# Splitting the gates' logarithms into two float32r numbers for the prefix sums of a gated linear attention

## The chip, the core and the metric

The kernel runs on one core of a Trainium2 chip. A core has five engines, each with its own instruction queue: PE (matrix products; its weight loads are listed apart as PEld), DVE (VectorE, elementwise work and reductions), ACT (ScalarE, activation functions and copies), POOL (GpSimd, some elementwise work and DMA issue) and SP (SyncE, DMA issue here). The metric is the device time of one execution in microseconds (us), the median over runs. Less is better.

## The reference

A linear attention with a forget gate feeds a mixture of experts with two levels of gates. Cut to what matters here:

```python
# q, k, v, f_logit: (4 batches, 8 heads, 768 steps, 48)
f = 1.0 / (1.0 + np.exp(-f_logit))
for t in range(S):
    state = f[:, :, t, :, None] * state + np.einsum('bhd,bhe->bhde', k[:, :, t], v[:, :, t])
    y[:, :, t] = np.einsum('bhd,bhde->bhe', q[:, :, t], state)
x = y.transpose(0, 2, 1, 3).reshape(3072, 384)
# 4 groups of 4 experts; each token goes to one group and one expert in it
h = np.maximum(x_of_expert @ w1[g, e], 0.0)      # 384 -> 1024
out[tokens] = weight * (h @ w2[g, e])            # 1024 -> 384
```

## The kernel before

**Stages.** The first 140 us or so are the attention stage, the rest the experts. Routing (which expert a token goes to) runs beside the attention, and the experts' weights are loaded while it ends.

**Units and passes.** The 768 steps are cut into 6 chunks of 128, the 4 batches into 2 pairs. A unit is a chunk and a pair: units 0 to 11, of 128 steps on the partitions and 2 x 8 x 48 = 768 columns. Inside a unit the recurrence is done with matrix products. They need, for each step, the sum of the logarithms of the gates from the chunk's first step to it. Unit i goes through these stages, each a Python generator whose yields split it into steps:

- c (`bounded`, L577): DVE clamps the loaded f logits in place (L581).
- g (`gated`, L584): ACT takes Exp (L591), then Ln (L594), so that `nl` holds the negative logarithm of the gate. Then, for each of the two batches, PE multiplies by the upper triangle `tri` of ones, which makes the sums over steps, `cs` (L600, a float32 product of 128x128 with 128x384), and ACT takes two Exps of it, `eq` (L601) and `kh` (L602). After the second batch a small DMA (L607) writes `ends`.
- m (`multiplied`): DVE multiplies q by `eq` (L620) and makes `kh` from it and k (L623).
- t (`turned`): PE transposes both (L634), ACT copies them out (L635).
- s (`scored`): PE makes the scores `ap` (L659), DVE masks them with `tri` into `am` (L662).
- n (`stated`): PE makes the state's increment `ds` (L676); DVE updates the state (`sp` L682, `st` L683).
- w (`weighed`): PE makes the outputs (L697 from the state, L701 from `am`), ACT copies them (L704).
- d, x, b: the gates' logits (`lT` L717, `lgT` L719, `lg` L722, `lgs` L723), the rows of x (L742 to L750), and the decays (`gt` L643, `decays` L644).
- r: one step of the routing of the oldest finished chunk (`route`, L178). Its DVE chain makes, among others, `pick` (L211), the places `at` (L220), `ln` (L226), `val` (L233), `meta` (L244) and `table` (L256). PE takes `val` in `tb` (L251). POOL sends `meta` by DMA (L246).

**Order.** The order on PE, DVE, ACT and SP is written out by hand: the sequence of steps is the order in which each of these engines gets its instructions, and each queue runs in that order. POOL's instructions are placed by the scheduler. A list `BEGIN` starts the first units. From `BEGUN = 3` to 11, pass i runs the list for i (`EVEN` or `ODD`, or an entry of `ORDERS`); a token such as `g+1` means the next step of stage g of unit i+1. In pass i the clamp of unit i+2 comes right after the masks of unit i, its Exp and Ln come between the later steps, and the sums of unit i+1 (`g+1 g+1`) come before the masks:

```python
EVEN = "l+2 d-2 n-1 r r r x-1 x-1 t t t t g+1 g+1 x-1 r s s s s c+2 w d-1 g+2 w g+2 n m+1 m+1".split()
```

So the sums of unit 5, the sixth, run in pass 4, and those of unit 11 in pass 10. Routing's chain from `pick` to `table` lies in the even passes.

**Loads.** Token `l+2` of pass i makes SP ask for k and q of unit i+2, f of unit i+3 and v of unit i+2 (L575). The tile of f has three buffers, and so the load of f of a unit waits until the unit three before has no further reader.

Of the kernel before, what the change touches and what calls it, by code (L numbers as in the profile page):

```python
# [10 lines left out]
FP32 = mybir.dt.float32  # L11
I32 = mybir.dt.int32
U32 = mybir.dt.uint32
BF16 = mybir.dt.bfloat16
AF = mybir.ActivationFunctionType
OP = mybir.AluOpType
AX = mybir.AxisListType.X
ET = mybir.EngineType
P = 128
# [4 lines left out]
def kernel(  # L24
# [12 lines left out]
    nc = tc.nc  # L37
    B, H, S, D = q.shape
# [38 lines left out]
    def const(shape, dtype, name):  # L77
        return cp.tile(shape, dtype, tag=name, name=name)

    def bank(shape, name):  # L80
        return ps.tile(shape, FP32, tag="bank", name=name)
# [7 lines left out]

    tri = const([P, P], FP32, "tri")  # L90
    ident = const([P, P], FP32, "ident")
    strictb = const([P, P], BF16, "strictb")
    onesb = const([P, P], BF16, "onesb")
    halves = const([P, 2], FP32, "halves")
    make_upper_triangular(nc, tri, val=1.0, diag=True)
    make_identity(nc, ident)
    nc.vector.memset(onesb, 1.0)
    nc.vector.tensor_tensor(strictb, tri, ident, OP.subtract)


# [43 lines left out]
    part = const([P, NC, B, 2], FP32, "part")  # L144
    partb = const([P, NC, B, 2], BF16, "partb")

# [23 lines left out]
    def rows_of(c, s=0, n=B):  # L170

        first = 1 + (c * B + s) * P
        return x_dram[first:first + n * P, :].rearrange("(b p) w -> p b w", p=P)
# [4 lines left out]
    def route(c, lg, sb, tabled=True, tidy=None, counted=None, ranking=None):  # L178


        def tmp(shape, name, dtype=FP32, bufs=1):
            return sb.tile(shape, dtype, tag=name, bufs=bufs, name=name)
# [13 lines left out]
        ohv = oh.rearrange("p (n a) e -> p n a e", n=B)  # L196
        ohe = tmp([P, B, GE], "ohe", BF16)
        nc.vector.tensor_tensor(ohe.rearrange("p n (g e) -> p n g e", e=EG), ohv[:, :, 1:G + 1, :],
# [5 lines left out]
        for n in range(B):  # L204
            nc.tensor.matmul(rk[:, n + 1:, :], lhsT=onesb, rhs=ohe[:, n:n + 1, :].broadcast_to((P, B - n, GE)), start=False, stop=(n == B - 1), skip_group_check=True)
        nc.scalar.activation(dl, dl, AF.Exp)
        yield
# [10 lines left out]
        if tabled:  # L218
# [5 lines left out]
            nc.vector.tensor_copy(atf, at)  # L224
            ln = tmp([P, B, P], "ln", BF16)
            nc.vector.tensor_tensor(ln, lanes.unsqueeze(1).broadcast_to((P, B, P)), atf[:, :, 0:1].broadcast_to((P, B, P)), OP.is_equal)  # L226
# [3 lines left out]
            nc.vector.tensor_tensor(head, heads_of.rearrange("p e j -> p (e j)").unsqueeze(1).broadcast_to(BLK), atf[:, :, 1:2].broadcast_to(BLK), OP.is_equal)  # L230
            val = tmp([P, 2, B, 2 * GE], "val", BF16)
            for m in range(2):
# [199 lines left out]
    def up(w, w1):  # L432
        n = w["n"]
        w["h"] = h = room(w, FO, "h")
        for f in range(0, FO, 2):
            hp = bank([P, 2, n], "hp")
            for o in range(2):
                for ko in range(KO):
                    nc.tensor.matmul(hp[:, o, :], lhsT=w1[:, ko, (f + o) * P:(f + o + 1) * P], rhs=w["xT"][:, ko, :], start=(ko == 0), stop=(ko == KO - 1))  # L439
            nc.scalar.activation(h[:, f:f + 2, :], hp, AF.Relu)  # L440
            yield

    def put(w, j, m, yp):

        y = w["pool"].tile([P, DM], FP32, tag="yt", bufs=2 if w["pool"] is ep else 4, name="yt")
        if w["n"] == P or "rows" in w:
            nc.scalar.activation(y[0:m], yp[0:m], AF.Copy, scale=w["x"][0:m, j, DM:DM + 1])  # L447
        else:
# [70 lines left out]
    with ExitStack() as fast:  # L519
        sb = fast.enter_context(tc.tile_pool(name="sb", bufs=2))  # L520
# [26 lines left out]
        NU = len(units)  # L547

        CORNERS = [(b, h) for b in range(2) for h in range(2)]
        KEPT = NU - 4  # L550
        live = {}
        groups, ends = {}, {}

        def heads(t):
            return t.rearrange("p b h d -> p (b h) d")

        def side(i):


            return nc.gpsimd if i < NU - 2 else nc.scalar  # L560
# [3 lines left out]
        def parts(i):  # L564

            return (slice(0, 1), slice(1, 2)) if i == 0 else (slice(0, 2),)

        def load(i, names):
            c, s = units[i]
            w = live.setdefault(i, {"v": pads["v"][i % 4], "qh": pads["qh"][i % 3]})  # L570
            for nm in names:
                if nm not in w:
                    w[nm] = sb.tile([P, 2, H, D], FP32, tag="ld_" + nm, bufs=3 if nm == "f" else 2, name="ld_" + nm)
                for b in parts(i) if nm == "f" else (slice(0, 2),):
                    nc.sync.dma_start(out=heads(w[nm][:, b])[:, :, 0:D], in_=SRC[nm][2 * s + b.start:2 * s + b.stop, :, c * P:(c + 1) * P, :].rearrange("b h t d -> t (b h) d"))  # L575
# [8 lines left out]
        def gated(i):  # L584

            c, s = units[i]
            w = live[i]

            nl = w["f"].rearrange("p b h d -> p b (h d)")
            for b in parts(i):  # L590
                nc.scalar.activation(nl[:, b], nl[:, b], AF.Exp, bias=0.0, scale=-1.0)  # L591
                if i:
                    yield
                nc.scalar.activation(nl[:, b], nl[:, b], AF.Ln, bias=1.0, scale=1.0)  # L594
            eq, qh, kh = pads["eq"][i % 2], w["qh"], pads["kh"][i % 3]
            w.update(eq=eq, kh=kh)
            yield
            for b in range(2):
                cs = bank([P, H, D], "cs")
                nc.tensor.matmul(cs.rearrange("t h d -> t (h d)"), lhsT=tri, rhs=nl[:, b], start=True, stop=True)  # L600
                nc.scalar.activation(eq[:, b, :, 0:D], cs, AF.Exp, bias=0.0, scale=-1.0)  # L601
                nc.scalar.activation(kh[:, b, :, 0:D], cs, AF.Exp, bias=0.0, scale=1.0)  # L602
                if b:

                    if s == 0:
                        ends[c] = sb.tile([B * HP, P], FP32, tag="ends", bufs=1, name="ends")
                    side(i).dma_start(out=ends[c][2 * HP * s:2 * HP * (s + 1), :], in_=eq[P - 1:P].rearrange("o b (a r) d -> o (b a) (r d)", r=2))  # L607
                yield
# [120 lines left out]
        def listed(i):  # L729

            c, s = units[i]
            xT = live[i]["xT"]
            if i < KEPT:
                if i % 4 == 0:
# [4 lines left out]
            for b in range(2):  # L739
# [8 lines left out]
                yield  # L748
            if i >= KEPT:
                side(i).dma_start(out=rows_of(c, 2 * s, 2)[:, :, 0:DM], in_=x.rearrange("t b a r d -> t b (a r d)"))  # L750
# [4 lines left out]
        def send_kept():  # L755

            for j, t in enumerate(rows_kept):
                nc.sync.dma_start(out=rows_of(2 * j, 0, 2 * B)[:, :, 0:DM], in_=t)
# [20 lines left out]
        def advance(gens):  # L779
            if gens and next(gens[0], True):  # L780
                gens.pop(0)
# [5 lines left out]

        STAGES = {"c": bounded, "g": gated, "m": multiplied, "t": turned, "s": scored, "n": stated, "w": weighed, "d": done, "x": listed, "b": decayed}
        BEGIN = """c0 g0 p g0 g0 m0 m0 m0 m0 l2 t0 t0 t0 t0 h c1 g1 g1 s0 s0 s0 s0 g1 g1 p w0 w0 n0 m1 m1 m1 m1 l3 h x0 x0 x0
            t1 t1 t1 t1 b1 c2 g2 g2 s1 s1 s1 s1 p d0 g2 g2 n0 n1 w1 w1 m2 m2 l4 n1  # L790
            d0 x1 x1 t2 t2 t2 t2 c3 g3 g3 x1 s2 s2 s2 s2 w2 g3 g3 d1 w2 n2 m3 m3 c4 g4 g4""".split()
        BEGUN = 3
        EVEN = "l+2 d-2 n-1 r r r x-1 x-1 t t t t g+1 g+1 x-1 r s s s s c+2 w d-1 g+2 w g+2 n m+1 m+1".split()
        ODD = "l+2 d-2 r r x-1 x-1 t t t t b n-1 g+1 g+1 x-1 r s s s s c+2 w d-1 g+2 w g+2 n m+1 m+1 r n".split()
        ORDERS = {
            NU - 3: "l+2 o d-2 r r x-1 x-1 t t t t b n-1 r g+1 g+1 x-1 r s s s s c+2 w d-1 g+2 w g+2 n m+1 m+1 r n".split(),
            NU - 2: "d-2 r x-1 x-1 r t t t t r g+1 g+1 x-1 s s s s w d-1 w n m+1 m+1".split(),
            NU - 1: "d-2 r r n-1 x-1 x-1 t t t t r x-1 r s s s s w b d-1 w r r".split(),
            NU: "d-2 r e d-1 x-1 x-1 d-1 x-1 r r r e e r e r r e r r e r e r r e e e e e".split(),
# [3 lines left out]
        def step(nm, i):  # L803
            if nm == "r":
                advance(routes)
            elif nm == "e":
                next(first[0], None)
            elif nm == "p":
                next(pad)
            elif nm == "o":  # L810
                send_kept()
            elif nm == "h":
                next(turning)
            elif 0 <= i < NU:
                if nm == "l":

                    load(i, ("k", "qh"))
                    if i + 1 < NU:
                        load(i + 1, ("f",))
                    load(i, ("v",))  # L820
                    return
                if (nm, i) not in steps_of:
                    steps_of[nm, i] = STAGES[nm](i)
                next(steps_of[nm, i], None)
# [14 lines left out]
        for i in range(BEGUN, NU + 1):  # L839
            if i == BEGUN:  # L840
                nc.sync.dma_start(out=x_dram[0:1, 0:DM].rearrange("o (h d) -> o h d", d=D), in_=blank[:, 0:D].unsqueeze(1).broadcast_to((1, H, D)))
                nc.sync.dma_start(out=x_dram[0:1, DM:RW], in_=blank[:, D:D + 2])
            for tok in ORDERS.get(i, ODD if i % 2 else EVEN):
                step(tok[0], i + int(tok[1:] or 0))
# [39 lines left out]
    ahead = {n: load_weights(wq if n % 3 == 1 else wp, who[0:1, PLACES[n]:PLACES[n] + 1]) for n in range(1, 2)}  # L884
# [22 lines left out]
    for n in range(GE - 1):  # L907
        w = ws[n]
# [105 lines left out]
    with tc.If(more > 0), ExitStack() as late:  # L1014
# [5 lines left out]
        with tc.For_i(0, last, 1) as i:  # L1020
            w1, w2 = load_weights(wp, b_expert[0:1, bass.ds(i, 1)])
# [13 lines left out]
            w = fetch(ep, row, P, late=True)  # L1035
# [32 lines left out]
```

## Time and profile before

| | us |
|---|---|
| median of 3 runs | 416.83 |
| the runs | 415.68 to 417.15 |
| the profiled execution, device time | 415.58 |
| its span in the trace | 413.8 |

| group (line, engine) | count | mean ns | busy us |
|---|---|---|---|
| `cs` product, L600 PE (two instructions a product) | 48 | 486 to 510 | 18.6 |
| expert product `hp`, L439 PE | 864 | 320 | 138.6 |
| expert product `yo`, L475 PE | 672 | 333 | 115.8 |
| masks `am`, L662 DVE | 48 | 682 | 29.8 |
| `qh` product, L620 DVE, 128x768, from 50 to 125 us | 7 | 949 | 6.6 |
| Exp, L591 ACT, 128x768, from 50 to 125 us | 6 | 844 | 5.1 |
| Ln, L594 ACT, 128x768, from 50 to 125 us | 6 | 849 | 5.1 |

A line of the profile's groups gives line, engine and operation, the tiles written and read, the shape, the count, then the busy time and the mean duration of one, and last the idle time of the engine before them with what ended it. Matrix products overlap each other, so their mean duration is longer than the distance between two of them. The timeline lists instructions of one engine by start and length; the chain of waits lists, in order of time, what the end of the program depended on. From 50 to 110 us PE was busy in every stretch of 10 us, DVE between 6.42 and 9.29 us of each, ACT between 6.81 and 7.39.

### The profile page before, as it was taken

The page shows a single profiled execution, that of the slowest core. Times are in us where ns is not written, and L with a number is a line of the kernel's source. Part 1 is how long each engine was busy: PE and PEld are TensorE (multiplying, and loading weights), DVE is VectorE, ACT ScalarE, POOL GpSimd, SP SyncE. Part 2 cuts the span into 40 slices and gives each one's busy share as a digit, 9 for nine tenths or more (in the row PEclk, how much of TensorE's full clock was granted, in tenths as well). Part 3 has the DMA queues.
Part 4 walks back from the last instruction along what each step waited for, and adds up shares of the span by engine and source line. Part 5 has one row for each costly group of instructions (what it writes and reads, how often), then busy time and mean ns, then how long its engine had stood idle before and what let it go on. Part 6 is the DMA issues. An engine that isn't in the chain of part 4 may idle for free.

```text
span 413.8 us, 10066 instructions
## 1 busy us (share of the span) xinstructions
PE 405.5 (98%) x4047; PEld 374.6 (91%) x4047; DVE 267.0 (65%) x778; ACT 157.1 (38%) x353; POOL 83.2 (20%) x127
## 2 busy tenths in 40 slices
PE   8999999999999999999999999999999999999995
PEld 3888888888778978889999999999999999999992
DVE  6666787878898722630899768486595595584230
ACT  6777766666565312221213122222232232231220
POOL 4000010101012157001042221311321320120230
PEclk9999999999999999999999999999999999999999
DMA  9999997877999559974829468486496596485010
GB/s 174 199 202 212 190 185 146 153 141 153 318 346 391 165 192 351 391 276 160 298 68 332 150 230 280 143 326 205 175 349 180 208 347 200 182 320 163 28 47 24
DMA packets 132145, 88.98 MB, mean 215 GB/s; under 512 B 102582, under 2 KB 122748, under 8 KB 132090
## 3 DMA queue, kind: packets, MB, share of 16 engines
q1 hardware_dynamic: 125666, 75.50, 62.1%
q0 software_dynamic: 5792, 11.92, 9.4%
q10 hardware_dynamic: 632, 0.83, 0.6%
q8 instruction: 34, 0.56, 0.5%
q14 instruction: 21, 0.17, 0.1%
HBM read 78.71 MB, written 9.83 MB: 214 GB/s over the span
## 4 chain that ended last, share of the span: by engine, by line
PE 48%; issue 30%; DMA 10%; POOL 6%; DVE 4%; POOLq 1%; ACT 1%; SPq 0%
PE hp L439 12%; DMA out_dram<-yt,xg 7%; PE yo L475 7%; PE ap L659 5%; PE y L701 5%; PE yo L460 4%; POOL out_dram L450 4%; PE cs L600 3%; POOL xg L393 2%; PE x_ps L742 2%; PE ds L676 2%; PE tr_k L634 2%; DMA xg<-x_dram,rows_e 2%; PE tr_q L634 2%; PE y L697 2%
## 5 line engine op out<-in xcount | busy, mean ns | idle before, releaser
L439 PE MATMUL hp<-xe,w 128*128 128x128 f32 (+14 forms) x864 | 138.6, 320 | 0.0
L439 PEld LDWEIGHTS hp<-xe,w 128*128 128x128 f32 x864 | 135.8, 190 | 0.8
L422 DVE STREAM_TRANSPOSE yr<-yT 32x192 f32<-32x192 f32 (+1 forms) x208 | 70.5, 339 | 70.4 <-ACT yT L476 67.8
L475 PE MATMUL yo<-h,w 128*128 128x230 f32 (+13 forms) x672 | 115.8, 333 | 0.0
L475 PEld LDWEIGHTS yo<-h,w 128*128 128x128 f32 x672 | 113.7, 190 | 0.2
L415 DVE STREAM_TRANSPOSE xe<-xg 32x192 f32<-32x192 f32 (+1 forms) x208 | 69.7, 335 | 8.6 <-PE hp L439 5.6
L440 ACT ACTIVATE h<-hp 128x256 f32<-128x256 f32 (+14 forms) x72 | 34.4, 478 | 103.5 <-PE hp L439 103.5
L450 POOL DMA_INDIRECT out_dram<-yt,xg x32 | 34.4, 1076 | 149.2 <-ACT yt L447 143.7
L476 ACT COPY yT<-yo 128x230 f32<-128x230 f32 (+13 forms) x42 | 13.5, 326 | 80.5 <-PE yo L475 80.5
L393 POOL DMA_INDIRECT xg<-x_dram,rows_p x30 | 29.6, 986 | 52.7 <-DMA out_dram<-yt,xg 29.7
L662 DVE TENSOR_TENSOR am<-ap,tri 128x512 f32<-128x512 f32 x48 | 29.8, 682 | 10.8 <-PE ap L659 10.8
L701 PE MATMUL y<-am,v 128*64 128x128 f32 x384 | 24.4, 276 | 0.2
L701 PEld LDWEIGHTS y<-am,v 128*64 128x64 f32 x384 | 20.9, 137 | 3.3 <-issue 1.8
L659 PE MATMUL ap<-Tq,Tk 48*64 48x128 f32 x768 | 23.8, 272 | 0.0
L659 PEld LDWEIGHTS ap<-Tq,Tk 48*64 48x64 f32 x768 | 20.8, 133 | 1.6 <-issue 1.1
L460 PE MATMUL yo<-w,h 128*128 128x384 f32 x64 | 21.3, 486 | 0.0
L460 PEld LDWEIGHTS yo<-w,h 128*128 128x128 f32 x64 | 11.9, 190 | 7.4
L600 PE MATMUL cs<-ld_f,tri 128*128 128x384 f32 x48 | 18.6, 510 | 0.0
L607 POOL DMA_DIRECT2D ends<-eq x10 | 5.4, 541 | 55.5 <-ACT eq L601 55.5
L447 ACT ACTIVATE yt<-yr,xg 128x384 f32<-128x384 f32 (+13 forms) x26 | 14.4, 604 | 5.4 <-DVE yr L422 5.4
L704 ACT COPY xT<-y 128x512 f32<-128x512 f32 x24 | 13.5, 581 | 4.5 <-PE y L701 4.4
L634 PE MATMUL tr_q<-ident,qh 128*128 128x128 f32 x96 | 14.5, 274 | 0.5 <-issue 0.5
(173 smaller groups left out, 369.5 us busy)
## 6 DMA issues: line engine op xcount, KB each, us to landing
w<-in_moe_w_dram SPq DMA_DIRECT2D x34, 1536.0 KB, 11.0
qh<-in_q_dram SPq DMA_DIRECT2D x12, 384.0 KB, 5.3
ld_k<-in_k_dram SPq DMA_DIRECT2D x12, 384.0 KB, 6.0
v<-in_v_dram SPq DMA_DIRECT2D x12, 384.0 KB, 5.8
ld_f<-in_f_logit_dram SPq DMA_DIRECT2D x11, 384.0 KB, 5.8
x_dram<-x_kept SPq DMA_DIRECT2D x2, 1536.0 KB, 11.1
x_dram<-x POOLq DMA_DIRECT2D x2, 384.0 KB, 6.9
x_dram<-x ACTq DMA_DIRECT2D x2, 384.0 KB, 8.1
```

The source lines that it names most:

```text
L393: nc.gpsimd.indirect_dma_start(out=w["x"][:, j, :], out_offset=None, in_=x_dram[0:1 + top, :], in_offset=bass.IndirectOffsetOnAxis(ap=rows ...
L415: squares(w, lambda n, k_, rk, g, rg: nc.vector.transpose(out=xT[rg, 0:n, k_], in_=x[rk, 0:n, g]))
L422: squares(w, lambda n, k_, rk, g, rg: nc.vector.transpose(out=y[rk, 0:n, g], in_=yT[rg, 0:n, k_]))
L439: nc.tensor.matmul(hp[:, o, :], lhsT=w1[:, ko, (f + o) * P:(f + o + 1) * P], rhs=w["xT"][:, ko, :], start=(ko == 0), stop=(ko == KO - 1))
L440: nc.scalar.activation(h[:, f:f + 2, :], hp, AF.Relu)
L450: sent = nc.gpsimd.indirect_dma_start(out=out, out_offset=bass.IndirectOffsetOnAxis(ap=w["x"][0:m, j, DM + 1:RW].bitcast(U32), axis=0), in ...
L460: nc.tensor.matmul(yp, lhsT=w["h"][:, fo, :], rhs=w2[:, fo, :], start=(fo == 0), stop=(fo == FO - 1))
L475: nc.tensor.matmul(yp, lhsT=w2[:, fo, m * P:(m + 1) * P], rhs=w["h"][:, fo, :], start=(fo == 0), stop=(fo == FO - 1))
L600: nc.tensor.matmul(cs.rearrange("t h d -> t (h d)"), lhsT=tri, rhs=nl[:, b], start=True, stop=True)
L634: nc.tensor.transpose(out=pt[:, a, :], in_=w[nm + "h"][:, b, 2 * a:2 * a + 2, :].rearrange("t r d -> t (r d)"), identity=ident)
L659: nc.tensor.matmul(ap[r][half, a, :], lhsT=w["Tk"][rows, b, a, half], rhs=w["Tq"][rows, b, a, :], start=True, stop=True)
L701: nc.tensor.matmul(ys[b][DP * h:DP * h + DP, a, :], lhsT=w["v"][:, b, 2 * a + (b ^ h), :], rhs=w["am"][b][:, b ^ h, a, :], start=(c == 0 a ...
```

## The change

From unit 5 on (`SPLIT = 5`), `nl` is split into two tiles of type float32r, in a step of its own: `most` is a rounded copy that ACT writes, `least` the rest, `nl - most`, that POOL writes. PE multiplies both by `trir`, the triangle as float32r, and adds the two products in the same `cs`. The tiles `most` and `least` have one buffer each. The constant `trir` is one more DVE copy at the start.

The order changes with it. In pass i the split of unit i+2 and Exp and Ln of unit i+3 stand before the masks (`g+2 g+3 g+3`), and the clamp of unit i+4 stands last (`c+4`), behind `qh` and `kh` of unit i+1. Pass 3 has a list of its own that catches up: clamps of units 5, 6 and 7, Exp and Ln of units 5 and 6, split of unit 5. The load of f moves a unit ahead: a new token `f6` stands in `BEGIN` behind `l4`, and from `l5` on the load of f is that of two units after, so that `l5` asks for f of unit 7.

```diff
@@ const
+    trir = const([P, P], F32R, "trir")
...
+    nc.vector.tensor_copy(trir, tri)
@@ gated
+            pieces = [nl]
+            if i >= SPLIT:
+                pieces = [sb.tile([P, 2, H * D], F32R, tag=nm, bufs=1, name=nm) for nm in ("most", "least")]
+                nc.scalar.copy(pieces[0], nl)
+                nc.gpsimd.tensor_tensor(pieces[1], nl, pieces[0].bitcast(FP32), OP.subtract)
+                yield
             for b in range(2):
                 cs = bank([P, H, D], "cs")
-                nc.tensor.matmul(cs.rearrange("t h d -> t (h d)"), lhsT=tri, rhs=nl[:, b], start=True, stop=True)
+                for n, piece in enumerate(pieces):
+                    nc.tensor.matmul(cs.rearrange("t h d -> t (h d)"), lhsT=trir if i >= SPLIT else tri, rhs=piece[:, b], start=(n == 0), stop=(n == len(pieces) - 1))
@@ orders
-            t1 t1 t1 t1 b1 c2 g2 g2 s1 s1 s1 s1 p d0 g2 g2 n0 n1 w1 w1 m2 m2 l4 n1
+            t1 t1 t1 t1 b1 c2 g2 g2 s1 s1 s1 s1 p d0 g2 g2 n0 n1 w1 w1 m2 m2 l4 f6 n1
-        EVEN = "l+2 d-2 n-1 r r r x-1 x-1 t t t t g+1 g+1 x-1 r s s s s c+2 w d-1 g+2 w g+2 n m+1 m+1".split()
-        ODD = "l+2 d-2 r r x-1 x-1 t t t t b n-1 g+1 g+1 x-1 r s s s s c+2 w d-1 g+2 w g+2 n m+1 m+1 r n".split()
+        EVEN = "l+2 d-2 n-1 r r r x-1 x-1 t t t t g+1 g+1 x-1 r g+2 g+3 g+3 s s s s w d-1 w n m+1 m+1 c+4".split()
+        ODD = "l+2 d-2 r r x-1 x-1 t t t t b n-1 g+1 g+1 x-1 r g+2 g+3 g+3 s s s s w d-1 w n m+1 m+1 c+4 r n".split()
         ORDERS = {
-            NU - 3: "l+2 o d-2 r r x-1 x-1 t t t t b n-1 r g+1 g+1 x-1 r s s s s c+2 w d-1 g+2 w g+2 n m+1 m+1 r n".split(),
+            BEGUN: "l+2 d-2 r r x-1 x-1 t t t t b n-1 g+1 g+1 c+2 x-1 r g+2 g+2 g+2 s s s s c+3 w d-1 g+3 w g+3 n m+1 m+1 c+4 r n".split(),
+            NU - 3: "l+2 o d-2 r r x-1 x-1 t t t t b n-1 r g+1 g+1 x-1 r g+2 s s s s w d-1 w n m+1 m+1 r n".split(),
@@ step
                 if nm == "l":
+                    ahead = i + 1 if i < BEGUN + 2 else i + 2
                     load(i, ("k", "qh"))
-                    if i + 1 < NU:
-                        load(i + 1, ("f",))
+                    if ahead < NU:
+                        load(ahead, ("f",))
                     load(i, ("v",))
                     return
+                if nm == "f":
+                    load(i, ("f",))
+                    return
```

More of the change, by code (lines that the diff above doesn't have):

```diff
@@ L14 @@
 BF16 = mybir.dt.bfloat16
+F32R = mybir.dt.float32r
 AF = mybir.ActivationFunctionType
@@ L550 @@
         KEPT = NU - 4
+        SPLIT = 5
         live = {}
```

## The prediction

> **What bounds the kernel now.** I read the page's first part, then the chain of waits from 40 to 125 us, then the timelines of DVE and SP where that chain leaves PE, then the groups by shape for prices. Busy shares first:
>
> ```profile
> PE 405.5 (98%) x4047; PEld 374.6 (91%) x4047; DVE 267.0 (65%) x778; ACT 157.1 (38%) x353; POOL 83.2 (20%) x127
> ```
>
> PE is the bound over the span, but a share is a mean over stages. The chain in the attention stage (columns: start, length, what) shows how thin the margin to DVE is:
>
> ```profile
> 51.87 1.29 PE cs L600 x4
> 53.16 0.12 PE tb L251 x4
> 53.28 1.91 PE ap L659 x64
> ...
> 73.14 1.29 PE cs L600 x4
> 74.43 0.12 PE tb L251 x4
> 74.55 1.91 PE ap L659 x64
> ...
> 115.88 0.56 DVE st L683
> 116.44 0.15 DVE lgs L723
> 116.58 0.21 DVE head L230
> 116.79 0.02 issue
> 116.82 0.51 DVE val L233 x2
> 117.32 0.05 issue
> 117.37 0.29 PE tb L251 x4
> ```
>
> Up to 102 us the chain is PE alone: each unit's cs costs 1.29 us (1.29 to 1.49). From 102.8 to 117.3 it is ACT and DVE, and PE waits at tb for val. The DVE timeline shows that even-numbered passes come close to this everywhere:
>
> ```profile
> 47.62 0.95 DVE L623 SCALAR_TENSOR_TENSOR kh<-kh,ld_k 128x768 f32<-128x768 f32 x1
> 48.49 0.21 DVE L211 TENSOR_TENSOR pick<-rk,run 128x64 f32<-128x64 f32 x1
> ...
> 52.16 0.49 DVE L233 TENSOR_TENSOR val<-head,part 128x128 bf16<-128x128 f32 x2
> ...
> 54.35 2.48 DVE L662 TENSOR_TENSOR am<-ap,tri 128x512 f32<-128x512 f32 x4 [0.27 <-PE ap L659]
> ```
>
> From 43.89 to 54.08 DVE never idles. val ends at 52.65 and PE's tb starts at 53.00 in the timeline: 0.35 us of slack, 0.30 after the 0.05 that the handover took at 117.3. The same gap stands at 74.27 and 95.68 (val ends 73.92 and 95.34). So whatever PE saves in an even pass beyond 0.30 us is given to waiting for val.
>
> **The change part by part.**
>
> *The sums.* Seven units (5 to 11) trade two float32 products for four float32r ones, each one instruction where float32 takes two. The trace has no float32r product. From above: the float32 instruction itself, 1.29/4 = 0.322 us for 384 columns; then four cost 1.29 and nothing is saved. From below: tb, bf16, 64 columns in 0.12/4 = 0.030 us, so 0.18 us for 384 and 0.72 for four. I take 0.18, since a rounded number read once resembles bf16 more than a float32 that is read twice: 0.57 us saved a unit, 4.0 over seven if PE were the bound throughout.
>
> [...]
>
> *The split.* ScalarE's copy is like L594, 128x768, 849 ns. It and the moved Exp and Ln (2.5 us together) fall into ACT's wait for lT (2.36 us idle before 67.51); lgT gets some 0.15 us late, hidden by the 0.71 us for which DVE waits for lg. Uncovered, that 0.15 would be paid a unit. GpSimd's subtraction is priced from the rows nearest to it:
>
> ```profile
> L890 POOL MEMSET yT<- 128x384 f32 x2 | 0.8, 442 | 0.0
> masks.py:199 POOL TENSOR_SCALAR_AFFINE_SELECT ident<-ident 128x128 f32<-128x128 f32 x1 | 0.3, 282 | 0.0
> ```
>
> 442/384 x 768 = 0.88 us, 282/128 x 768 = 1.69 us, and double that, 3.4, were each input to cost a pass. I take 1.7, as the select also reads SBUF. PE uses the result some 5 us later, so its own time is free. In POOL's queue the subtractions of units 6, 8 and 10 stand behind the DMA of meta (75.78) and ends (76.56), starting near 77.1, still 6 us before their use at 83.8; nothing urgent is behind them.
>
> What it may cost is DVE's. In pass 5 ACT ends dl's Exp at 65.15, the copy at 65.97, the subtraction at 67.67; earlier sums advance that by only the 0.17 us that eq waited for cs, to 67.50, while the masks (end 67.56) move by 0.57, to 66.99. If DVE's qh and kh products cannot run beside GpSimd, qh is c = 0.5 us late, in the odd passes, whose DVE chain runs straight into val. No row shows the two together: c lies between 0 and 0.5, and 2.2 with the 3.4 us subtraction. I take 0.5.
>
> [...]
>
> *The loads and the clamp.* Here I see the main cost. Pass 3 (42 to 53 us) must catch up two units: clamp 5 runs ahead of its masks (in 0.94 us of idle), clamp 6 after them, clamp 7 last, behind kh. The load of f 6 moves up, behind v 4; f 7 takes its place. The SP queue (columns: start, length) is full there, since it issues without a gap from 0.7 to 55 us:
>
> ```profile
> 38.05 1.46 SPq L575 DMA_DIRECT2D v<-in_v_dram  x1
> 39.61 1.71 SPq L841 DMA_DIRECT2D x_dram<-blank  x1
> 41.43 0.31 SPq L842 DMA_DIRECT2D x_dram<-blank  x1
> 41.84 0.39 SPq L575 DMA_DIRECT2D ld_k<-in_k_dram  x1
> 42.32 1.57 SPq L575 DMA_DIRECT2D qh<-in_q_dram  x1
> 43.99 1.86 SPq L575 DMA_DIRECT2D ld_f<-in_f_logit_dram  x1
> 45.91 2.86 SPq L575 DMA_DIRECT2D v<-in_v_dram  x1
> ```
>
> With f 6 put in at 39.6, f 7 has exactly the loads before it that v 5 has now; v 5 starts at 45.91 and lands after 6.0 us, so f 7 lands near 51.9. DVE reaches clamp 7 at 48.49 and, being in order, waits 3.4 us; clamp takes 0.47. Queued behind it are pick to val, 48.49 to 52.65 = 4.16 us. So val ends at 51.9 + 0.47 + 4.16 = 56.53, and PE's tb starts at 56.58, not 53.00: +3.58 us, with the sixth unit's saving swallowed. In later passes f is asked for 2 us after the previous kh ends (82.05 against 80.2), lands 5.8 us later, and is clamped after the next kh, 10 us on: no wait there.
>
> *Rest.* trir's copy (0.29 us by strictb's row) hides in DVE's 0.85 us wait for the first load; without that cover it is paid once. The last two units' clamps have left the DVE chain of passes 8 to 10.
>
> **The sum**, as PE's lateness against before: pass 4 +3.58; pass 5 -0.57; pass 6 -0.30 (val limits it) + 0.5 (c); pass 7 -0.57; pass 8 -0.29 + 0.5; passes 9 and 10, DVE-bound, keep nothing of cs 10 and lose unit 11's clamp, -0.47; cs 11 comes after tb, but PE then waits anyway (0.48 us at 133.68) for the gathered rows, whose time follows DVE's meta, so 0. From there PE is busy to the end. Total +2.38 us. The profiled run took 415.58 us with a span of 413.8; it becomes 418.0. The median, 416.83, lies 1.25 above, so on that scale the forecast is **419.2**.
>
> **The rivals.** (1) *No stall in pass 4.* For it: f 7's place is read off another kernel's queue, and 48 to 50 us shows DMA at only 0.49 of its share. Against: seven issues back to back. The +3.58 becomes -0.30, total -1.5, or -2.5 with c = 0: 414.3 to 415.3. This is the other side; it decides if f 7 lands before 48.5. (2) *float32r at 0.322 us.* Nothing saved; masks do not move, c falls to 0.1, within the slack of 0.30: 3.58 - 0.47 = +3.1, 419.9. So the rate of the new product moves the end by less than 1 us while the stall stands. (3) *GpSimd holds DVE.* Subtraction of 3.4 us, c = 2.2 in passes 5 and 7: +5.8, 422.6; it decides once the subtraction exceeds 2 us. (4) *Neither gain nor stall*: -0.47, 416.4.
>
> **How the numbers follow.** What one measurement can tell is about 0.5%, 2.1 us: below 414.75 is faster, above 418.9 slower. Forecast 0.44, its own range 418.2 (c = 0, +1.4) to 420.2: 0.26 slower, 0.18 same. Rival 1 0.30: 0.18 faster, 0.12 same. Rival 2 0.13: 0.11 slower, 0.02 same. Rival 3 0.08, slower. Rival 4 0.05, same. Sums: faster 0.18, same 0.37, slower 0.45. Range 414.2 to 421.2: it leaves out rival 3 and the tails.
>
> **What would show it.** In the changed profile: four cs instructions a unit at 0.72 us or less (else rival 2); DVE's clamp of unit 7 waiting some 3 us for ld_f near 49 to 52, then PE idle for as long before tb; the subtraction near 1.7 us and qh starting when it ends, not when the masks end; tb waiting for val again in passes 6 and 8. The prediction is wrong if f 7 has landed when DVE gets to it, or if DVE keeps ahead of tb in the even passes.

## The result and the profile after

| | before | after |
|---|---|---|
| median, us | 416.8 | 421.9 |
| the runs, us | 415.68 to 417.15 | 421.63 to 423.67 |
| the profiled execution, us | 415.58 | 421.69 |
| its span, us | 413.8 | 419.9 |

The ratio is 1.0136, with an interval of 1.0102 to 1.017: slower by 5 us. The forecast was 419.2, with 421.2 as the top of its range. First the busy shares of the page of the changed kernel:

```profile
PE 404.1 (96%) x4047; PEld 375.6 (89%) x4047; DVE 272.6 (65%) x779; ACT 163.0 (39%) x360; POOL 98.9 (24%) x134
```

PE is busy 1.4 us less than before, and the span is 6.1 longer: PE stands idle 7.5 us more. The chain of waits around pass 4 (start, length, what) answers to the lines shown of before:

```profile
45.77 6.13 DMA ld_f<-in_f_logit_dram
...
51.92 0.56 DVE ld_f L585
...
55.83 0.21 DVE head L233
...
56.06 0.51 DVE val L236 x2
56.57 0.05 issue
56.62 0.35 PE tb L254 x4
```

Here the chain was PE alone. Now it leaves PE for the load of f 7, goes on through its clamp and through all that DVE has queued behind it, to val, and comes back at tb, 3.62 us later than before (53.00 in the timeline). The timelines of DVE and of PE show who lost what (start, length; in brackets the idle time before the instruction and what ended it):

```profile
46.72 2.60 DVE L632 TENSOR_TENSOR qh<-qh,eq 128x768 f32<-128x768 f32 x1
49.23 0.95 DVE L635 SCALAR_TENSOR_TENSOR kh<-kh,ld_k 128x768 f32<-128x768 f32 x1
51.92 0.56 DVE L585 TENSOR_SCALAR ld_f<-ld_f 128x768 f32<-128x768 f32 x1 [1.74 <-DMA ld_f<-in_f_logit_dram]
```

```profile
53.26 0.66 PE L646 MATMUL tr_k<-ident,kh 128*128 128x128 f32 x4 [1.86 <-DVE run L217]
...
56.62 0.35 PE L254 MATMUL tb<-val,ln 128*128 128x64 bf16 x4 [1.93 <-DVE val L236]
56.90 3.52 PE L671 MATMUL ap<-Tq,Tk 48*64 48x128 f32 x64
```

DVE idles for f 7 for 1.74 us only, because qh before it took 2.60 us and not 0.95. PE idles twice, and then ap takes 3.52 us where it always took 1.98. The stretch of that ap in the windows (start and end, length, busy time of PE, PEld, DVE, ACT and POOL with instruction counts, granted clock, DMA share, which can come out above 1 for a short stretch, GB/s) says why:

```profile
57.00:58.00 1.00, 1.00 (x20) 1.00 (x24) 0.87 (x5) 0.97 (x2) 0.00 (x0) 0.50 1.26 234
```

PE does 20 of these products in a microsecond, at a granted clock of 0.50; from 57 to 61 us the mean clock is 0.61, and in the same stretch of before it is 1.00.

The second place is pass 9. DVE's copy `who`, of 1x2 elements, was short before:

```profile
109.21 0.16 DVE L289 CAST who<-names 1x2 int32<-1x2 f32 x1
```

After, on POOL, DVE and PE:

```profile
113.30 1.81 POOL L607 TENSOR_TENSOR least<-ld_f,most 128x768 fp32r<-128x768 f32 x1 [4.03 <-ACT most L606]
```

```profile
113.56 1.56 DVE L292 CAST who<-names 1x2 int32<-1x2 f32 x1
115.04 2.47 DVE L674 TENSOR_TENSOR am<-ap,tri 128x512 f32<-128x512 f32 x4
```

```profile
115.77 0.43 PE L713 MATMUL y<-am,v 128*64 128x128 f32 x2 [1.86 <-DVE am L674]
```

`who` ends when GpSimd's subtraction ends. The masks stand behind it, and PE waits 1.86 us for them. The reduction `names` right before `who`, at 113.35, ran inside the same subtraction and took 0.17 us. The third place is the gather of the first experts' rows: PE waits 1.16 us for them at 139.55, where it waited 0.48 before.

The new products themselves are as fast as was hoped. In pass 5 a unit's four follow each other like this (the first is 0.28 us ahead of the second):

```profile
68.11 0.34 PE L612 MATMUL cs<-most,trir 128*128 128x384 f32 x1
68.28 0.34 PE L612 MATMUL cs<-least,trir 128*128 128x384 f32 x1
```

Put together, from the starts of tb and ap in the two timelines, as the changed kernel's lateness against before in us:

| stretch | predicted | measured |
|---|---|---|
| tb of pass 4 | +3.58 | +3.62 |
| tb of pass 4 to ap of pass 5 | -0.57 | +1.04 |
| to ap of pass 6 | +0.20 | +0.10 |
| to ap of pass 7 | -0.57 | -0.51 |
| to ap of pass 8 | +0.21 | +0.11 |
| to tb of pass 10 | -0.47 | +0.93 |
| to the transposes of the gathered rows | 0 | +0.58 |
| to the end of the span | 0 | +0.23 |
| sum | +2.38 | +6.10 |

The second row is -0.57 plus 1.61 of half clock (1.54 in ap, 0.07 in tb). The sixth is 1.40 us away from the prediction, which is the 1.40 by which `who` grew.

### The profile page after: what moved, and what is told of

Its sections match the earlier page's. It is cut to its first block, busy times and chain, and to the rows that moved or that the text cites. A ratio compares the mean times of both kernels' runs of the same rounds, so it can differ in the third digit from the quotient of the medians.

```text
span 419.9 us, 10089 instructions
## 1 busy us (share of the span) xinstructions
PE 404.1 (96%) x4047; PEld 375.6 (89%) x4047; DVE 272.6 (65%) x779; ACT 163.0 (39%) x360; POOL 98.9 (24%) x134
## 4 chain that ended last, share of the span: by engine, by line
PE 42%; issue 30%; DMA 10%; DVE 9%; POOL 6%; ACT 1%; POOLq 1%; DVEq 0%
PE hp L442 12%; PE yo L478 6%; DMA out_dram<-yt,xg 6%; PE ap L671 5%; PE yo L463 4%; POOL out_dram L453 4%; PE y L713 3%; POOL xg L396 2%; DMA ld_f<-in_f_logit_dram 2%; PE cs L612 2%; PE x_ps L754 2%; DMA xg<-x_dram,rows_e 2%; DVE am L674 2%; PE tr_k L646 1%; PE tr_q L646 1%
## 5 line engine op out<-in xcount | busy, mean ns | idle before, releaser
L671 PE MATMUL ap<-Tq,Tk 48*64 48x128 f32 x768 | 25.3, 284 | 0.0
L671 PEld LDWEIGHTS ap<-Tq,Tk 48*64 48x64 f32 x768 | 22.4, 140 | 1.1 <-ACT decays L656 0.3
L632 DVE TENSOR_TENSOR qh<-qh,eq 128x768 f32<-128x768 f32 (+1 forms) x14 | 15.7, 1121 | 1.7 <-ACT eq L613 1.7
L646 PE MATMUL tr_k<-ident,kh 128*128 128x128 f32 x96 | 14.4, 274 | 1.9 <-DVE run L217 1.9
```

Of the source, the lines that this page charges most:

```text
L646: nc.tensor.transpose(out=pt[:, a, :], in_=w[nm + "h"][:, b, 2 * a:2 * a + 2, :].rearrange("t r d -> t (r d)"), identity=ident)
L671: nc.tensor.matmul(ap[r][half, a, :], lhsT=w["Tk"][rows, b, a, half], rhs=w["Tq"][rows, b, a, :], start=True, stop=True)
```

## The experiments

The theory: (a) f 7's late landing stalls DVE, val and tb; (b) the idle time of PE that this makes halves its clock; (c) GpSimd's subtraction holds some of DVE's instructions, `who` in pass 9 and qh elsewhere; (d) the gather adds the rest. The rivals stand with each experiment. The runs were made in five groups on different chips, on which the kernel before took 416.8, 421.8, 422.3, 416.3 and 416.9 us. So only ratios to the kernel before beside them are compared between groups, and times inside a trace.

**The clamp of unit 7 later**, in pass 4 and not last in pass 3 (second group):

```diff
-            BEGUN: "... s s s s c+3 w d-1 g+3 w g+3 n m+1 m+1 c+4 r n".split(),
+            BEGUN: "... s s s s c+3 w d-1 g+3 w g+3 n m+1 m+1 r n".split(),
+            BEGUN + 1: "... g+1 g+1 x-1 r g+2 c+3 g+3 g+3 s s s s w d-1 w n m+1 m+1 c+4".split(),
```

> The changed kernel, but the clamp of unit 7 is no longer last in pass 3: it stands in pass 4, behind routing's steps and before the masks. Theory (f 7's late landing holds DVE, then val and tb, and the two idle stretches of PE that it makes halve the clock): DVE no longer waits for f 7. But the product qh of unit 4, which took 2.60 us beside GpSimd's subtraction, still makes kh end at 50.1 instead of 48.5; 50.1 + 4.16 = 54.3, so tb starts at 54.4, not 56.6 (before the change: 53.0), and ap of pass 4 takes 1.9 us at full clock, not 3.46. Saved: 2.2 + 1.55 = 3.8 us of the changed kernel's time, so 417.9 on the scale of its profiled 421.69. Rival 1 (the half clock has another cause than PE's idle time): ap still takes 3.4 us, saved 2.2, 419.5. Rival 2 (the stall does not reach the end, since the gather of the first experts' rows sets it): saved under 1 us, 421 or more.

Measured: ratio 1.0066 (1.0034 to 1.0099), so about half of the loss is back. In the trace it is 1.9 us, against the changed kernel's trace of the third group, in which the clock fell in the same two passes: at tb of pass 4 (54.60, not 56.47) and still at tb of pass 10 (121.25, not 123.12). The timelines of DVE and PE:

```profile
47.01 2.59 DVE L632 TENSOR_TENSOR qh<-qh,eq 128x768 f32<-128x768 f32 x1
```

```profile
54.60 0.28 PE L254 MATMUL tb<-val,ln 128*128 128x64 bf16 x4 [1.56 <-DVE val L236]
54.81 2.75 PE L671 MATMUL ap<-Tq,Tk 48*64 48x128 f32 x64
```

tb starts at 54.60, as worked out (54.4): the stall is gone, and what stays late is what the subtraction took from qh, which the stall had covered. One point of the theory failed: the clock still dropped (0.50 from 56 to 59 us), now after an idle time of 1.56 us. It fell later, so ap lost only 0.77 us, but the y products behind it took 1.95 us and not 1.05, and from ap of pass 4 to ap of pass 5 the whole 1.6 us is still there (11.85 against the 10.24 that the sums' saving leaves of before's 10.81).

**PE kept busy ahead of tb**, with the stall left in (second group):

```diff
-            tb = bank([P, 2, GE, 2], "tb")
+            tb = bank([P, 8 * 2 * GE * 2], "tb")
+            if c == 0:
+                for _ in range(8):
+                    nc.tensor.matmul(tb, lhsT=onesb, rhs=onesb.unsqueeze(1).broadcast_to((P, 4, P)), start=True, stop=True)
+            tb = tb[:, 0:4 * GE].rearrange("p (m e j) -> p m e j", m=2, j=2)
```

> The changed kernel with eight bf16 products of 128x512 (0.22 us each at full clock, 1.8 us together) put on PE right ahead of the first tb, into tb's own bank, which tb then overwrites. They fill PE's second idle stretch before tb (54.5 to 56.6) and change nothing else. Theory (the idle time makes the clock drop): tb still starts near 56.6, the granted clock stays above 0.9 from 56 to 60 us, ap takes 1.9 instead of 3.46 us; 421.69 - 1.55 = 420.1. Rival (the clock drop comes from something else, as the DMA load or the products' kind): ap still takes 3.4 us, 421.7.

Measured: ratio 1.011 (1.0072 to 1.0149), and PE's timeline is:

```profile
54.33 1.90 PE L255 MATMUL tb<-onesb 128*128 128x512 bf16 x8
56.40 0.28 PE L258 MATMUL tb<-val,ln 128*128 128x64 bf16 x4 [0.18 <-DVE val L236]
```

tb is as late as ever, ap takes 1.98 us, and the clock stands at 1.00 from 57 to 61. The DMA share from 57 to 58 is 1.28, as in the changed kernel (1.26), and the case of the order alone below kept its clock from 57 to 61 with a higher share (0.96) than the changed kernel (0.87), so the half clock does not go with the DMA share. The time itself tells nothing here: the interval of 1.011 overlaps that of the changed kernel. The trace fits (b), but alone it doesn't settle it, since two other kernels with the stall kept their clock too (the order alone and unit 11 unsplit, 1.00 from 57 to 61). The traces of all kernels together say more: in the attention stage PE had an idle stretch of over 1.2 us in pass 4 in nine of them (1.56 to 2.48 us, the longest of each) and in pass 9 in five (1.85 or 1.86). After 10 of these 14 the granted clock fell; from pass 4 to pass 10 it fell nowhere else. So no drop came here without such idle time, and it did not always bring one: the four places without a drop had 1.65, 1.75, 1.86 and 1.92 us.

In the changed kernel's trace the clock stood at 0.50 for 3.41 us, from 56.71 to 60.12. In seven of the ten places the windows lose as much clock as some 3.4 us at 0.50 (the mean is 0.87 from 52 to 65 us in this trace and in that of the later clamp), in the three others as much as some 6.8 us (0.74 from 52 to 65 us in the last kernel below). In stretches of that length, counted from 56.71, PE of the changed kernel was idle for 1.86 us from 49.88 to 53.30, and the clock stayed at 1.00 behind it; for 1.93 us from 53.30 to 56.71, and the drop followed; and for 0.82 and 1.32 us in the two stretches across which the gap of pass 9 lies (111.32 to 118.15), and it stayed at 1.00. That is one trace; what decides whether a gap brings a drop is not shown.

**No subtraction** after unit 5's (second group). The low part of the logarithms is left out; the second product's operand is a tile of zeros:

```diff
...
-                nc.gpsimd.tensor_tensor(pieces[1], nl, pieces[0].bitcast(FP32), OP.subtract)
+                if not zero:
+                    zero.append(sb.tile([P, 2, H * D], F32R, tag="least", bufs=1, name="least"))
+                    nc.gpsimd.tensor_tensor(zero[0], nl, nl, OP.subtract)
+                pieces.append(zero[0])
```

> GpSimd's subtraction runs once, for unit 5, as nl - nl; that tile of zeros is the second operand of the sums of units 5 to 11. Left out is the low part of the logarithms; PE, ACT, DVE and all loads have the same instructions. Theory (GpSimd's subtraction holds DVE's instructions): who in pass 9 takes 0.16 us instead of 1.56 and the masks of pass 9 start 1.4 us earlier; qh takes 0.95 us in passes 5 to 8 instead of 1.34 and 1.8. Saved 1.4 in pass 9 and up to 0.4 each in passes 5 and 7: 1.4 to 2.2 us, 419.5 to 420.3. The stall of pass 4 with ap at 3.4 us stays. Rival (who waits for something else there, such as a DMA issue or a register load): who still 1.5 us, no more than 0.8 saved, 420.9 or more.

Measured: ratio 1.0106 (1.0055 to 1.0158). DVE's timeline in pass 9:

```profile
113.69 0.16 DVE L292 CAST who<-names 1x2 int32<-1x2 f32 x1
113.77 2.47 DVE L678 TENSOR_TENSOR am<-ap,tri 128x512 f32<-128x512 f32 x4
```

`who` takes 0.16 again, and qh 0.95 in every pass. From ap of pass 5 to ap of pass 6 it is 10.17 us and not 10.56: the subtraction's price c on DVE in an odd pass is 0.39. From ap of pass 8 to tb of pass 10 it is 21.00 us, where it was 21.48 before and 22.41 in the changed kernel: without the subtraction this stretch comes out as the prediction had it (-0.47). Theory (c) stands, the rival falls.

**The order alone**, with no unit split (second group):

```diff
-        SPLIT = 5
+        SPLIT = 99
...
+            if i >= 5 and i < SPLIT:
+                yield
             if i >= SPLIT:
```

> The new order, loads and clamps, but no unit is split: ACT's copy, the subtraction and the float32r products are gone, and the sums of all units are float32 products again. Theory (the order carries the loss): tb of pass 4 starts at 56.5 or later, DVE waits 3.4 us for f 7, ap takes 3.4 us; +3.6 + 1.55 in pass 4, nothing in passes 5 to 8, -0.5 in passes 9 and 10: +4.7 us against before, 420.3 on the scale of its profiled 415.58. Then the split and its products cost 1.4 us in the changed kernel, in all. Rival (the split carries the loss): within 1 us of before, 416.6 or less.

Measured: ratio 1.0098 (1.0056 to 1.0139), tb of pass 4 at 56.42. In the profiled execution the clock held after the stall (1.00 from 57 to 61). So the order by itself costs some 1% here. The split, which was to save, does not win that back; whether it adds to the loss can't be told, since the interval overlaps that of the changed kernel.

**The third group** has the changed kernel again, and three others. First the changed kernel as it is:

> The changed kernel itself, beside the three others of this group, since the chip of the second group of runs need not be that of the first. Every theory: slower than before by 1.0 to 1.7%, with tb of pass 4 near 56.6 us and who of pass 9 at 1.5 us. It is what the other three are measured against.

Measured: ratio 1.0142 (1.0108 to 1.0177), tb of pass 4 at 56.47, `who` 1.56. Here the clock also fell in pass 9 (a mean of 0.83 from 110 to 120 us), behind the 1.86 us for which PE waited for the masks.

Then the same with unit 11 unsplit:

```diff
-            if i >= SPLIT:
+            if i >= SPLIT and not (SPLIT <= i < NU - 1):
+                yield
+            if SPLIT <= i < NU - 1:
...
-                    ... lhsT=trir if i >= SPLIT else tri, ...
+                    ... lhsT=trir if SPLIT <= i < NU - 1 else tri, ...
```

> The changed kernel, but unit 11 is not split (units 5 to 10 are), so that no subtraction runs on GpSimd in pass 9, and the sums of unit 11 are float32 products again. Theory: who takes 0.16 us and the masks of pass 9 start 1.4 us earlier; tb of pass 10, measured from ap of pass 8, comes 1.4 us earlier than in the changed kernel; the 0.58 us that the sums of unit 11 then cost come after tb, where PE waits for the gathered rows anyway: 1.4 us less, ratio to the changed kernel 0.997. Rival (the gather's time is set by the load of the experts' weights and the writes of x, not by DVE's chain): tb 1.4 us earlier, but the gathered rows land no earlier, ratio 1.000.

Measured: ratio 1.014 (1.0104 to 1.0176). `who` is 0.16, and tb of pass 10 comes 20.99 us after ap of pass 8 where it was 23.18 in the changed kernel beside it (with the half clock of pass 9 in it). But the gather starts 32.17 after that ap where it was 32.57: 2.2 us gained on DVE and PE, 0.4 left at the gather. The rival's numbers came: something else than DVE's chain sets the gather.

**Only units 6, 8 and 10 split, no stall** (the first experiment's order, and the condition of the last one changed in each of its three places):

```diff
-            if SPLIT <= i < NU - 1:
+            if i in (6, 8, 10):
```

> The version that should be the best: the clamp of unit 7 in pass 4 as in the first experiment, and only units 6, 8 and 10 split, whose subtractions fall in the even passes 4, 6 and 8 (where qh has time) and whose float32r sums fall in the odd passes 5, 7 and 9 (where PE, not val, sets the pace). Theory: tb of pass 4 at 53.0 and ap there 1.9 us, so no stall and no half clock; ap of pass 5 minus ap of pass 4 and the same from 6 to 7 are 0.5 shorter than before, the even passes as before; unit 11's clamp gone from pass 9, -0.5; in all 1.5 us under before, ratio to before 0.996. Rival 1 (the saved PE time is given back where DVE's chain sets the end): within 0.3 us of before, ratio 1.000. Rival 2 (something in the new loads or order costs time that the stall hid): slower than before, 1.003 or more.

Measured: ratio 0.9996 (0.997 to 1.0022). The mechanism came as expected: tb of pass 4 at 53.18, ap 1.98, passes 5, 7 and 9 shorter by 0.57 to 0.72, tb of pass 10 at 115.78 against 117.37. But the gather starts at 126.78, where before has 126.47 (and 127.43 in its second trace, below), 9.2 us after the issue of meta. PE stops twice near 129 us with no wait that the trace shows, which takes 1.7 us, and still waits 0.46 us for the gathered rows. So by then the gain is gone, as rival 1 said, but not to DVE's chain, which was ahead. In this trace the clock also fell near 170 us (a mean of 0.84 from 160 to 170 and 0.82 from 170 to 180).

**The same order with no split at all** (the edits of the first experiment and of the order alone together):

> The new order and loads with the clamp of unit 7 in pass 4, and no unit split: what the order alone is worth once its stall is gone. Theory: tb of pass 4 at 53.0, passes 5 to 8 as before, pass 9 half a microsecond less (the clamp of unit 11 is gone from it): 0 to 0.5 us under before, ratio 0.999; and against the order with the stall and no split (1.0098 to before) some 1.1% less. Rival (the early clamps and the moved loads cost time of their own): slower than before by 0.5% or more.

Measured: ratio 0.997 (0.9944 to 0.9995), with tb of pass 4 at 53.01. So the new order and loads cost nothing once the stall is out; they may gain a little.

What sets the gather? A candidate: in POOL's queue the small write of `meta`, for which the gather waits, stands behind the 384 KB of x of unit 9, which the first gather does not read. The fourth group moves x of unit 9 to SP's queue, and takes `who` out of the subtraction's way:

```diff
-                side(i).dma_start(out=rows_of(c, 2 * s, 2)[:, :, 0:DM], ...
+                (nc.sync if i == 9 else side(i)).dma_start(out=rows_of(c, 2 * s, 2)[:, :, 0:DM], ...
```

> The kernel before, unchanged, for its trace beside the others of this group, since no trace of it stands beside theirs yet: ratio 1.000. What it tells: whether PE's short stops without a wait near 130 us and the drop of the granted clock near 170 us, which the changed kernels show in the second and third group of runs, belong to the chip (then they are here too) or to the change (then they are not).

Measured: 1.0005 (0.9988 to 1.0022). Its trace has neither the stops near 130 us nor the drop near 170; in the other two kernels of this group one stop of 0.16 and one of 0.43 us is left. So the change does not bring them by itself. For half clock in general the record says the same of the other chips: in the second and third group 7 of 12 and 17 of 23 runs of the kernel before have a mean granted clock of 0.995 or less, and none has in the fourth and fifth group. Near 170 us, too, the drops stand beside idle time. In six traces of the second and third group PE was idle for 1.85 to 2.83 us between 160 and 180 us, and the mean clock from 170 to 180 was 0.74 to 0.83; in the traces of the fourth and fifth group, and in the first ones of before and of the changed kernel, PE was busy all through these 20 us, and the clock stayed at 1.00. What makes the stops is open.

The kernel with units 6, 8 and 10 split, and x of unit 9 moved:

> The version with units 6, 8 and 10 split and no stall, and one edit more: the rows x of unit 9 are written by SP's queue and not by POOL's, where they stand ahead of the small write of meta for which the gather of the first experts' rows waits. Theory (the 1.6 us that this version is ahead of before at tb of pass 10 is given back at the gather, because meta lands behind x in one queue): the gather starts 6 us after the issue of meta and not 9.2, near 124; PE no longer waits for it (0.46 us), and the time is at most 0.5 us lower than without the edit, since PE's own stops near 130 us come next: ratio to before 0.997 to 0.999. Rival (the gather waits for the rows of units 0 to 7 or for the experts' weights that fill the DMA engines): the gather stays at 126 to 127, nothing changes, ratio 1.000.

Measured: ratio 0.9949 (0.9934 to 0.9965), 414.12 against 416.25 us: faster than the kernel before, by more than was expected. POOL's timeline:

```profile
117.53 0.78 POOL L249 DMA_DIRECT2D x_dram<-meta  x1 [13.62 <-DVE mine L318]
124.66 1.08 POOL L396 DMA_INDIRECT xg<-x_dram,rows_e  x1 [6.35 <-DVE oh L198]
```

From meta's issue to the gather it is 7.1 us, where it was 9.2 without this edit (on another chip), and PE takes the gathered rows at 131.83 without a wait.

The other kernel of the group is the changed one with that edit and this:

```diff
-        nc.vector.reduce_sum(out=names, in_=which, axis=AX)
-        nc.vector.tensor_copy(who[:, 0:np_], names)
+        nc.vector.tensor_reduce(out=who[:, 0:np_], in_=which, axis=AX, op=OP.max)
```

> The changed kernel, with who written by a reduction (max) straight into int32 in place of a reduction and a copy, and x of unit 9 in SP's queue as in the run beside it. The subtraction of unit 11 stays where it is. Theory (GpSimd's subtraction holds only some forms of DVE's instructions: the copy, and products of two inputs in SBUF, but not a reduction): who ends in 0.2 us beside the subtraction, the masks of pass 9 start at once, tb of pass 10 comes 1.4 to 2.5 us earlier, measured from ap of pass 8 (22.4 in the changed kernel, 21.0 then), and with the gather out of the way 1.5 us or more of the 1.4% come back: ratio 1.008 to 1.011. Rival 1 (any DVE instruction at that place is held): the reduction takes 1.5 us, nothing changes, 1.014. Rival 2 (the gather stays): tb earlier, ratio 1.012 to 1.014.

Measured: ratio 1.0063 (1.0042 to 1.0083). POOL's and DVE's timelines:

```profile
113.43 1.81 POOL L606 TENSOR_TENSOR least<-ld_f,most 128x768 fp32r<-128x768 f32 x1 [4.03 <-ACT most L605]
```

```profile
113.50 0.17 DVE L291 TENSOR_REDUCE who<-which 1x2 int32<-1x32 f32 x1
113.60 2.46 DVE L673 TENSOR_TENSOR am<-ap,tri 128x512 f32<-128x512 f32 x4
```

The reduction runs in 0.17 us in the midst of the subtraction; in the changed kernel the copy took 1.56 us there and ended with it. tb of pass 10 comes 20.83 us after ap of pass 8. With the two edits together half of the loss is back, without any change to the split.

**The queue alone** (fifth group), on the kernel before and on the changed one:

> The kernel before with one edit: x of unit 9 in SP's queue and not in POOL's ahead of meta. It is the control of the best version, which has the same edit. Theory: the gather starts 1 to 2 us earlier, PE's wait for its rows (0.48 and 1.30 us in the two traces of before) is gone; ratio 0.997 to 0.999, and of the best version's 0.9949 a half is left to the three split units. Rival 1 (without the split the edit moves nothing, since DVE's chain sets the gather): 1.000. Rival 2 (the edit gives it all): 0.995.

Measured: 0.9979 (0.9965 to 0.9993); the gather starts 6.9 us after meta's issue (7.3 and 8.6 in the two traces of before) and PE does not wait for it. In the eleven traces with x ahead of meta the gather starts 6.8 to 9.4 us after meta's issue, in the four without 6.9 to 7.6: the edit takes the long ones away, but the queue is not all that sets this time.

It also leaves open what the three split units are worth at the end. The order with no split had 0.997 and the queue's edit 0.9979; multiplied, they give the 0.9949 of the best version, and that version without the split was not run. For the split speak the traces: PE takes the gathered rows at 131.83 there and at 134.12 here, 0.70 us of which is a stop without a wait. That is one trace each, on two chips.

> The changed kernel with that same edit alone. It tells apart what is still open of the loss: the gather started 0.8 us later than the lateness of DVE's chain explains, and PE waited 1.16 us there. Theory (meta lands behind x in one queue, and the later x is, the more of the weights' transfers it shares the engines with): the gather starts 6 to 7.3 us after the issue of meta and not 8.3, PE's wait falls from 1.16 to under 0.3 us; 1 us less, ratio 1.011 to 1.012. Rival (PE's lateness in passes 4 and 9 is all of the loss and its wait at the gather only a remainder of it): ratio 1.0136 as before.

Measured: 1.0139 (1.0111 to 1.0167). The gather starts 7.6 us after meta's issue (8.3 in the changed kernel) and PE's wait is gone, but no time is won: in its profiled execution the clock fell in pass 9 as well as in pass 4 (means of 0.89 from 110 to 125 us and 0.74 from 52 to 65), and its runs spread from 420.98 to 424.31 us. A microsecond can't be told in them. Nor does the trace show that the edit took the wait away, since the half clock of pass 9 made PE itself later: in the third group's trace of the changed kernel, with that half clock and x still ahead of meta, the wait was already down to 0.21 us. So neither is shown for the changed kernel, that PE waits there because of the queue's order, or that this costs it 0.6 us.

## Why the prediction was right about the stall and too low

- *f 7 lands near 51.9, val ends at 56.53, tb starts at 56.58.* Right to 0.04 us (51.90, 56.57, 56.62), with two small errors that cancel: the clamp took 0.56 us and not 0.47, pick to val 4.09 and not 4.16. The place of f 7, read off the SP queue of the kernel before, held. One thing under it was missed: qh of unit 4 ran beside unit 5's subtraction and took 2.60 us. The wait covered it; without the wait it costs 1.6 us by itself, which the later clamp laid bare.
- *float32r at 0.18 us a product.* Right: after the first, the products follow each other at 0.175 to 0.18 us, and cs of a unit takes 0.79 to 0.90 us where it took 1.29 to 1.49. Rival 2 is out. Pass 7 got 0.51 of the 0.57; in pass 5 the half clock covers it.
- *The subtraction at 1.7 us, c = 0.5.* The subtraction takes 1.81 to 1.85 (2.02 for unit 5). The 0.5 was the upper end of the author's estimate, which no row of before could narrow; c is 0.39 in passes 5 and 7, and in the even passes qh's 1.8 us are hidden. Rival 3, a subtraction of 3.4 us, is out. The masks, which read PSUM, run beside it in 2.48 us (69.82 in pass 5), as ever.
- *Rival 1, no stall.* Its condition failed (f 7 landed 3.4 us after 48.5), and its price was too good for this split: with the stall out, qh in pass 3 and `who` in pass 9 remain. Rival 4, neither gain nor stall, falls with it.
- *The step that failed: "passes 9 and 10, DVE-bound, keep nothing of cs 10 and lose unit 11's clamp, -0.47".* They came out at +0.93. The working gave c to passes 5 and 7 and looked for it at qh and kh alone. In pass 9 the chain of `less` to `who` lies ahead of the masks, so the subtraction met a copy there, which it held for 1.4 us. The case without the subtraction, where this stretch is -0.48, and the reduction beside it show it.
- *The term that was left out: the clock.* The +3.58 was priced as lateness alone. Behind PE's idle time of 1.86 and 1.93 us the clock fell to 0.50, which cost 1.61 us in the profiled execution. Of the two terms, 1.40 and 1.61, each alone would have left the time within the range, whose top is 421.2.
- *"cs 11 comes after tb, but PE then waits anyway: 0."* PE waits there, but this stretch came out at +0.58. The working had the rows follow DVE's meta; the gather started 8.3 us after meta's issue, and 7.3 in the kernel before. That x ahead of meta in the queue makes this difference fits the runs, but is not shown for the changed kernel.
- *The scale.* The 1.25 us added to go from the profiled execution to the median were not there after: 421.69 profiled, 421.9 the median. So of the 3.7 us that the sum missed in the trace 1 us does not show in the medians, by luck.

## What to carry to other kernels

A wait on the bounding engine had two prices here, the lateness (3.62 us) and the half clock behind it (1.61 us); where a change opens gaps like these in PE's work, put the second into the sum as well, with its chance (10 of 14 places with a gap of over 1.2 us here, some 1.6 us in most). Before giving GpSimd a pass over a tile, lay its span over every DVE instruction in that stretch, the tiny ones too, and ask which it holds; here the copy, of 1.56 us beside the subtraction, could be written as a reduction of 0.17. And where several stages hand over through one DMA queue, see what stands ahead of the small transfer on which the next stage waits (here from meta's issue to the gather it was 6.8 to 9.4 us with x ahead of it, and 6.9 to 7.6 without).

## What the runs showed of the hardware

- DVE's product qh (two inputs in SBUF, 0.95 us alone) took from 1.34 to 2.60 us where it met GpSimd's subtraction of 1.8 to 2.0 us, and the copy `who`, of 1x2 elements and 0.16 us alone, 1.56 us. The masks (one input in PSUM, 2.48 us for the four) and the reduction that makes `names` (0.17 us) took no longer beside it.
- The granted clock fell to 0.50 behind 10 of 14 places in which PE had a gap of over 1.2 us, the shortest of them a single gap of 1.56 us. In the changed kernel's trace the drop lasted 3.41 us, from 56.71 to 60.12. A drop of that length cost PE some 1.6 us, one of some 6.8 us up to 3.2 (from ap of pass 4 to ap of pass 5 it was 13.43 us in the last kernel of the study, 11.78 in the changed one's first trace, and 10.24 with no drop).
- Float32r products of 384 columns followed each other at 0.175 to 0.18 us on PE, four to a unit; the float32 instruction of 384 columns took 0.322 us, and each product was two of them.
